# Reordering the first pair's attention, and the loads around it, in a retention-plus-mixer kernel

## The chip, the cores and the metric

The kernel runs on one core of one Trainium2 chip. The metric is the device time of one execution in microseconds (us), as the median of several runs, and lower is better. Each run also lists its mean granted TensorE clock, and 1.0 is full speed.

Short names: PE is the tensor engine, DVE VectorE, ACT ScalarE, POOL GpSimd, SP SyncE. q0 is the DMA queue that POOL's transfers use (the casting loads of the weights w1 and w2, and the stores of the output), q1 the one that SP's transfers use (loads of q, k, v, and the transposing DMAs).

## The reference

```python
# q, k, v: (8, 8, 576, 64); U: (576, 32); V: (32, 576); w_ch1: (512, 2048); w_ch2: (2048, 512)
scores = scale * np.matmul(q, k.transpose(0, 1, 3, 2))
gamma = 1.0 - 2.0 ** (-5.0 - np.arange(H))
Dmat = np.where(rel >= 0, gamma[:, None, None] ** rel[None], 0.0)   # rel = i - j
attn = np.matmul(scores * Dmat, v)
x = attn.transpose(0, 2, 1, 3).reshape(B, S, H * D)                 # (8, 576, 512)
u = x + (x.transpose(0, 2, 1) @ U @ V).transpose(0, 2, 1)           # mixing over the sequence
out = u + np.maximum(u @ w_ch1, 0.0) @ w_ch2                        # expansion, then contraction
```

## The kernel before

Batches are handled in pairs. The first pair's attention, with nothing before it to hide behind, is written out by hand in `startup` and `first_stretch`, in four units of 256 positions and two half tiles called J. From about 55 us on, a merged list runs: the two big matrix products of one pair on PE, with the attention of the next pair's chunks between them. A chunk is prepared by loads on q1, casts, and one transposing DMA:

```python
def load(pr, i, which):                     # q1: loads of a chunk's q, k, v
    ...
            nc.sync.dma_start(out=c["f", j][rows, :, :], in_=dram[...])
def xbar(pr, i):                            # q1: the chunk's transposing DMA, its output is qkT
    nc.sync.dma_start_transpose(
        out=c["qkT"], in_=c["qk"].rearrange("p j n -> p (j n)"))
def load_w1(f0, f1):                        # q0, as is load_w2
    nc.gpsimd.dma_start(out=w1_sb[:, :, w], in_=moe_w_ch1[:, w].rearrange(...))
def SC(c, pp):                              # scores of a chunk: needs qkT
    ...
            nc.tensor.matmul(pp[...], qkT[...], qkT[...], start=True, stop=True)
```

The end of the startup has the two halves of unit 1's output in one PSUM tile, with a copy (`XS_u`) after each state product (`QS_u`):

```python
RV_u(1, 1)
QS_u(1, 0, 1)
XS_u(1, 0, 1)
ST_u(1, ALL, acc2, False)
Sblk(acc2, 3)
QS_u(1, 1, 2)
XS_u(1, 1, 2)
```

In the first stretch, `y(n)` issues n expansion groups (u times a slice of w1, line L515), and w2 is loaded whole:

```python
for g in range(NI, NI + 4):                 # four chunks of the next pair
    load(*order[g], (1, 0, 2) if g < NI + 3 else (1, 0))
unit(2, (0, 1, 2), False)
y(2)
unit(3, (2, 3), True)
nc.vector.memset(w2_sb[:, 0, 0:1], 0.0)     # a marker: the loads stand behind it
for f in range(0, NF, 2):
    load_w2(f)
```

The lines named below: L514/L515 is the expansion with w1, L548/L549 the contraction with w2, L295/L296 the scores of a later chunk, L278/L279 the transposing DMA, L242/L243 the chunk loads. The lower number is with the change.

Of the kernel before, what the change touches and what calls it, by code (L numbers as in the profile page):

```python
# [9 lines left out]
FP32 = mybir.dt.float32  # L10
BF16 = mybir.dt.bfloat16
AF = mybir.ActivationFunctionType
# [22 lines left out]
def kernel(  # L35
# [11 lines left out]
    nc = tc.nc  # L47

    B, H, S, D = q.shape
    dm = H * D  # L50
# [66 lines left out]
    def early_consts():  # L117
# [26 lines left out]
        for h in range(H):  # L144
# [10 lines left out]
        nc.vector.tensor_tensor(out=posJ, in0=posJ, in1=lngt[:, 0:2, :], op=ALU.mult)  # L155
        nc.scalar.activation(out=vscaleJ, in_=posJ, func=AF.Exp, bias=lnb, scale=-1.0)
        nc.scalar.activation(out=posJ, in_=posJ, func=AF.Exp, bias=0.0, scale=1.0)
        nc.vector.tensor_scalar(
            out=triU[0:HALF], in0=iotaU[0:HALF], scalar1=0.0, scalar2=None, op0=ALU.is_ge)
        nc.vector.tensor_scalar(  # L160
# [4 lines left out]
        nc.vector.tensor_tensor(out=lngt, in0=lngt, in1=pos, op=ALU.mult)  # L165
        nc.scalar.activation(out=qscale, in_=lngt, func=AF.Exp, bias=0.0, scale=1.0)
        nc.scalar.activation(out=vscale, in_=lngt, func=AF.Exp, bias=lnb, scale=-1.0)
        nc.vector.tensor_copy(out=triH[0:HALF], in_=tri[0:HALF, 0:HALF])
        nc.vector.tensor_copy(out=triH[HALF:P], in_=tri[HALF:P, HALF:P])
        nc.vector.memset(U_E[:, J, :], 0.0)  # L170
        nc.vector.memset(U_O[0:HALF, 0, :], 0.0)
        nc.vector.memset(V4[:, 0:HALF], 0.0)
        nc.vector.memset(V4[:, HALF + S:], 0.0)
        nc.vector.tensor_copy(out=swap[:, 0:HALF], in_=ident[:, HALF:P])
        nc.vector.tensor_copy(out=swap[:, HALF:P], in_=ident[:, 0:HALF])

    def load_u_rows():
        nc.sync.dma_start(
# [53 lines left out]

    ch = {}

    def load(pr, i, which):
        c = ch.setdefault((pr, i), {})
        for j in which:
            if ("f", j) not in c:
                c["f", j] = stage.tile([P, H, D], FP32, tag="stage", name="stage_t")
            dram = (q, k, v)[j]  # L240
            for rows, b, t0 in parts(pr, i):
                n = rows.stop - rows.start  # L242
                nc.sync.dma_start(  # L243
                    out=c["f", j][rows, :, :],
                    in_=dram[b, :, t0:t0 + n, :].rearrange("h s d -> s h d"),
                )
# [383 lines left out]
    def cast_u(u, j, hh, eng):  # L630
        o, f = unit_views(u, j, hh)
        if eng is nc.scalar:
            nc.scalar.activation(out=o, in_=f, func=AF.Copy)
        else:
            eng.tensor_copy(out=o, in_=f)  # L635
# [145 lines left out]
    def zero_J(x, eng):  # L781
        for j in range(3):
            t = stage.tile([P, H, D], FP32, tag="stage", name="stage_t")
            hj[x]["f", j] = t
            if eng is nc.scalar:
                nc.scalar.activation(
                    out=t.rearrange("p h d -> p (h d)"),
                    in_=ident[:, None, :].to_broadcast([P, 4, P]), func=AF.Copy, scale=0.0)
            else:
                eng.memset(t, 0.0)  # L790
# [6 lines left out]
                out=hj[x]["f", j][0:P:2], in_=src.rearrange("h s d -> s h d"))  # L797

    def cast_J(x, eng_k, eng_q):
        t = qk_pool.tile([P, 2, dm], BF16, tag="qk", name="qk")  # L800
        hj[x]["qk"] = t
        for j, e in ((1, eng_k), (0, eng_q)):
            f = hj[x]["f", j]
            if j == 0 and x == 0:
                e.tensor_tensor(
                    out=t[:, 0, :].rearrange("p (h d) -> p h d", d=D), in0=f,
                    in1=posJ[:, 0, :, None].to_broadcast([P, H, D]), op=ALU.mult)
            elif e is nc.scalar:
                nc.scalar.activation(
                    out=t[:, j, :], in_=f.rearrange("p h d -> p (h d)"), func=AF.Copy)  # L810
            else:
                e.tensor_copy(out=t[:, j, :], in_=f.rearrange("p h d -> p (h d)"))
# [96 lines left out]
    def startup():  # L909
# [12 lines left out]
        cast_unit(0)  # L922
        T_u(0, 1, nc.vector)
        nc.vector.memset(un[0]["off"][HI], 0.0)
        zero_J(1, nc.vector)
        load_J(1, (1, 0, 2))
        load_u(2, (1, 0, 2))
# [7 lines left out]
        cast_unit(1)  # L935
        cast_u(0, 2, 0, nc.gpsimd)
        cast_u(0, 2, 1, nc.gpsimd)
        cast_u(1, 2, 0, nc.gpsimd)
        load_w1(0, 2)
        cast_u(1, 2, 1, nc.gpsimd)  # L940
        T_u(1, 1, nc.scalar)
        SC_u(0, 1, ps_o, "po")
        mask_u(0, 1)
        SC_off(0, ps_sc, "psc")
        warm(3)
        T_u(1, 0)
        nc.vector.memset(sblk, 0.0)
        SC_off(1, ps_o, "po")
        warm(3)
        SC_u(1, 0, ps_sc, "psc")  # L950
        mask_u(1, 0)
        cast_J(0, nc.scalar, nc.vector)
        SC_u(1, 1, ps_o, "po")
        mask_u(1, 1)

        acc1 = pss_tile()
        ST_u(0, ALL, acc1, True)
        Sblk(acc1, 1)
        RV_u(0, 0)
        RV_u(0, 1)  # L960
        RV_off()
        XS_u(0)
        T_J(0)
        acc2 = ps_big.tile([P, NHP, P], FP32, tag="big", name="pss2")
        ST_u(0, ALL, acc2, True)
        prep_vJ(0)
        cast_urows()
        RV_u(1, 0)
        SC_J(0)
        mask_J(0)  # L970
        ST_u(1, LO, acc1, False)
        Sblk(acc1, 2)
        cast_J(1, nc.gpsimd, nc.gpsimd)
        load_w1(2, 4)
        prep_vJ(1)
# [6 lines left out]
        load_w1(8, 10)  # L982
        for hh in range(2):
            cast_u(2, 2, hh, nc.gpsimd)
        load_w1(10, 14)
        scale_u(3, 0, nc.gpsimd)
        for hh in range(2):
            cast_u(3, 0, hh, nc.gpsimd)
        load_w1(14, 16)
        for hh in range(2):  # L990
            cast_u(3, 2, hh, nc.gpsimd)
        RV_u(1, 1)
        QS_u(1, 0, 1)
        XS_u(1, 0, 1)
        ST_u(1, ALL, acc2, False)
        Sblk(acc2, 3)
        QS_u(1, 1, 2)
        XS_u(1, 1, 2)
        RV_J(0)
        QS_J(3)  # L1000
        XS_J(0)

        xT = [ps_big.tile([P, dm], FP32, tag="big", name="xT") for _ in range(3)]
        xT.append(ps_sc.tile([P, dm], FP32, tag="psc", name="xT"))

# [27 lines left out]
    def first_stretch():  # L1033
# [21 lines left out]

        def unit(u, slots, last):
            T_u(u, 1, nc.vector)
            if last:
                y(1)
            T_u(u, 0)  # L1060
            y(1)
            SC_u(u, 0, ps_sc, "psc")
            mask_u(u, 0)
            y(1)
            ST_u(u, LO, acc, False)
            Sblk(acc, slots[1])
            SC_u(u, 1, ps_sc, "psc")
            mask_u(u, 1)
            if not last:
                scale_u(3, 1, nc.vector)  # L1070
            y(1)
            if not last:
                ST_u(u, HI, acc, False)
                Sblk(acc, slots[2])
            RV_u(u, 0)
            QS_u(u, 0, slots[0])
            QS_u(u, 1, slots[1])
            if last:
                RV_J(1)
                XS_J(1)  # L1080
            RV_u(u, 1)
            XS_u(u)

        for g in range(NI, NI + 4):
            load(*order[g], (1, 0, 2) if g < NI + 3 else (1, 0))
        unit(2, (0, 1, 2), False)
        y(2)
        unit(3, (2, 3), True)
        nc.vector.memset(w2_sb[:, 0, 0:1], 0.0)
        for f in range(0, NF, 2):  # L1090
            load_w2(f)
        y(1)
        MA1()
# [11 lines left out]
        Y1(2, 0)  # L1105
        for f in range(3):
            Y1(f, 1)
        return rest[3:]

    with tc.manual_schedule():  # L1110
# [58 lines left out]
```

## Time and profile before

| | before |
|---|---|
| median of 3 runs | 326.29 us (325.11 to 327.68) |
| span in the profile | 323.8 us |
| PE busy | 312.6 us, 97% |
| granted clock | 1.00 |
| first expansion group | 24.49 us |
| first contraction group | 72.98 us |

A line of the timeline reads: start, length, engine, line, operation, output from inputs, sizes, how many, and in brackets the idle time before it with what ended it. This is the PE timeline of before from 60 us:

```profile
59.79 6.99 PE L515 MATMUL ps_y<-uT,w_sb 128*128 128x256 bf16 x49
66.71 0.32 PE L296 MATMUL pp<-qkT 64*64 64x64 bf16 x16
...
69.64 2.77 PE L515 MATMUL ps_y<-uT,w_sb 128*128 128x256 bf16 x20 [0.65 <-ACT y L520]
...
72.98 3.19 PE L549 MATMUL ps_y<-w_sb,y 128*128 128x512 bf16 x14
```

### The profile page before, as it was taken

What the parts mean: (1) busy time and instruction counts of PE and PEld (TensorE: products, weight loads), DVE (VectorE), ACT (ScalarE), POOL (GpSimd) and SP (SyncE); (2) the same over time, 40 slices, a digit from 0 to 9 for tenths busy, and PEclk for the clock granted to TensorE, in tenths of its full rate; (3) what the DMA queues carried; (4) which work ended last, traced back from release to release, by engine and by line L of the source; (5) the groups of instructions that cost most, each with busy time, mean ns of one, the idle gap of its engine ahead of it and who ended that gap; (6) DMA issues with size and microseconds to landing.
All of it is one profiled execution on the core that took longest, in us unless ns stands there. A gap on an engine that the chain in (4) does not pass through costs nothing.

```text
span 323.8 us, 9143 instructions
## 1 busy us (share of the span) xinstructions
PE 312.6 (97%) x3885; PEld 170.8 (53%) x3885; DVE 172.9 (53%) x342; ACT 146.1 (45%) x334; POOL 101.5 (31%) x172
## 2 busy tenths in 40 slices
PE   7899899999999999999999999999999999999996
PEld 3575545764444454457644454457644454467544
DVE  7867456229726577555844476556744475500012
ACT  6757547892020583058800583058800572047400
POOL 7796329223113723052221523052231500010000
PEclk9999999999999999999999999999999999999999
DMA  7999999999975999979997599959996340330022
GB/s 215 256 233 255 227 216 185 201 188 127 254 180 139 232 193 187 213 147 190 197 205 166 140 184 206 217 140 189 182 217 156 100 68 3 107 105 0 2 78 84
DMA packets 152904, 53.30 MB, mean 165 GB/s; under 512 B 132032, under 2 KB 150336, under 8 KB 152864
## 3 DMA queue, kind: packets, MB, share of 16 engines
q1 hardware_dynamic: 144512, 40.40, 68.1%
q0 software_dynamic: 8352, 12.32, 15.9%
q8 instruction: 30, 0.49, 0.7%
q14 instruction: 10, 0.08, 0.1%
HBM read 36.85 MB, written 9.44 MB: 143 GB/s over the span
## 4 chain that ended last, share of the span: by engine, by line
PE 77%; ACT 4%; DVE 2%; DMA 1%; issue 1%; DVEq 0%
PE ps_y L549 37%; PE ps_y L515 32%; PE pp L296 2%; DVE u L464 2%; ACT y L520 1%; DMA qkT<-qk 1%; PE pp L316 1%; PE pp L328 1%; PE ps_y L560 1%; PE AB L358 1%; PE pa L431 1%; PE ph L458 1%; ACT s_sb L373 1%; ACT qk L264 0%; ACT uT L489 0%
## 5 line engine op out<-in xcount | busy, mean ns | idle before, releaser
L515 PE MATMUL ps_y<-uT,w_sb 128*128 128x256 bf16 (+2 forms) x768 | 133.1, 326 | 1.8 <-ACT y L520 1.1
L520 ACT ACTIVATE y<-ps_y 128x384 bf16<-128x384 f32 (+2 forms) x192 | 89.7, 491 | 96.6 <-PE ps_y L515 95.8
L549 PE MATMUL ps_y<-w_sb,y 128*128 128x512 bf16 x560 | 126.5, 380 | 0.0
L515 PEld LDWEIGHTS <-w_sb 128*128 128x128 bf16 x768 | 72.1, 98 | 49.6 <-issue 3.7
L549 PEld LDWEIGHTS <-y 128*128 128x128 bf16 x560 | 52.6, 98 | 61.1
L272 POOL TENSOR_TENSOR vt<-stage_t,vscale 64x256 bf16<-64x256 f32 (+1 forms) x81 | 50.4, 622 | 63.8 <-DMA stage_t<-in_v_dram 51.8
L538 DVE TENSOR_TENSOR o_sb<-ps_y,u 128x512 f32<-128x512 f32 (+2 forms) x38 | 25.2, 664 | 81.7 <-PE ps_y L549 79.4
L541 POOL DMA_DIRECT2D out_dram<-o_sb x31 | 17.2, 555 | 103.7 <-DVE o_sb L538 100.0
L304 DVE TENSOR_TENSOR ret<-pp,triH 128x512 bf16<-128x512 f32 x27 | 18.7, 692 | 24.6 <-PE pp L328 19.1
L464 DVE TENSOR_TENSOR u<-ph,xt 128x768 bf16<-128x768 f32 (+2 forms) x24 | 21.8, 951 | 5.9 <-PE ph L458 4.2
L437 ACT ACTIVATE a_sb<-pa 128x128 bf16<-128x128 f32 x8 | 2.2, 278 | 43.7 <-PE pa L431 43.7
L344 DVE TENSOR_TENSOR xt<-pp,qscale 128x512 bf16<-128x512 f32 x27 | 18.6, 690 | 4.7 <-PE pp L328 4.2
L338 DVE COPY q<-qkT 64x256 bf16<-64x256 bf16 x48 | 13.1, 272 | 13.7 <-DMA qkT<-qk 12.7
L263 DVE CAST qk<-stage_t 64x256 bf16<-64x256 f32 x54 | 18.8, 347 | 1.2
L383 DVE TENSOR_TENSOR s_sb<-AB,Af 64x256 bf16<-64x256 f32 x42 | 17.7, 422 | 2.1 <-ACT s_sb L378 1.5
L264 ACT ACTIVATE qk<-stage_t 128x512 bf16<-128x512 f32 x27 | 16.8, 622 | 0.0
L635 POOL CAST qk<-stage_t 128x512 bf16<-128x512 f32 x16 | 10.2, 637 | 11.4 <-DMA stage_t<-in_q_dram 6.6
L376 ACT ACTIVATE Af<-AB 128x256 f32<-128x256 f32 x24 | 9.2, 385 | 7.8 <-PE AB L358 7.4
L261 ACT ACTIVATE qk<-stage_t 128x256 bf16<-128x256 f32 x27 | 11.1, 410 | 0.0
L692 DVE TENSOR_TENSOR ret<-psc,triU 128x1024 bf16<-128x1024 f32 x8 | 9.6, 1206 | 2.6 <-PE psc L684 2.6
L296 PEld LDWEIGHTS <-qkT 64*64 64x64 bf16 x432 | 5.6, 107 | 9.8 <-issue 8.0
L209 PE MATMUL pw<-ident 128*128 128x512 bf16 x26 | 7.8, 443 | 1.4 <-POOL ident masks.py:199 1.4
(134 smaller groups left out, 220.0 us busy)
## 6 DMA issues: line engine op xcount, KB each, us to landing
stage_t<-in_k_dram SPq DMA_DIRECT2D x32, 256.0 KB, 4.9
stage_t<-in_q_dram SPq DMA_DIRECT2D x32, 256.0 KB, 5.4
stage_t<-in_v_dram SPq DMA_DIRECT2D x32, 256.0 KB, 5.6
out_dram<-o_sb POOLq DMA_DIRECT2D x31, 256.0 KB, 3.5
w_sb<-in_moe_w_ch_dram POOLq DMA_DIRECT2D x14, 256.0 KB, 8.3
stage_t<-in_k_dram SPq DMA_DIRECT2D x8, 128.0 KB, 3.7
stage_t<-in_q_dram SPq DMA_DIRECT2D x8, 128.0 KB, 3.7
stage_t<-in_v_dram SPq DMA_DIRECT2D x8, 128.0 KB, 3.9
```

What stands on the lines that cost most here:

```text
L263: nc.vector.tensor_copy(out=o[to, hl], in_=f[fr, hl])
L264: nc.scalar.activation(out=c["qk"][:, 0, :], in_=c["f", 0].rearrange("p h d -> p (h d)"), func=AF.Copy)
L272: nc.gpsimd.tensor_tensor(out=o[to, hl], in0=f[fr, hl], in1=w[fr, hl, :, None].to_broadcast([n, NHP, D]), op=ALU.mult)
L304: nc.vector.tensor_tensor(out=ret.rearrange("p a b i -> p a (b i)").rearrange("p a (b i) -> p a b i", i=D), in0=pp[:, :, 0:NHP * D].rearra ...
L344: nc.vector.tensor_tensor(out=st["x", pr][:, i, :].rearrange("p (hp hl d) -> p hl hp d", hl=2, d=D), in0=pp[:, :, NHP * D:2 * NHP * D].rea ...
L383: nc.vector.tensor_tensor(out=S_[half(x), 1, :], in0=Bk[half(1 - x)], in1=Af[half(1 - x), now, :], op=ALU.add)
L464: nc.vector.tensor_tensor(out=st["u", par][:, i0 - base:i0 - base + n, w].rearrange("p s (c d) -> p c s d", c=2), in0=ph[k][:, :, 0:n, :], ...
L515: nc.tensor.matmul(ps[:, 0:n, :], w1_sb[:, cc, f * P:(f + 1) * P], st["uT", par][:, c0:c0 + n, cc, :], start=(cc == 0), stop=(cc == NCC - 1),)
L520: nc.scalar.activation(out=st["y1", par][:, f, c0 * P:(c0 + n) * P], in_=ps[:, 0:n, :].rearrange("p s t -> p (s t)"), func=AF.Relu)
L538: nc.vector.tensor_tensor(out=o_sb[:, 0:n], in0=ps[:, 0:n], in1=st["u", par][:, c, w], op=ALU.add)
L541: (nc.sync if last else nc.gpsimd).dma_start(out=out_flat[r0:r0 + P, w], in_=o_sb[:, 0:n])
L549: nc.tensor.matmul(ps, st["y1", par][:, f, c * P:(c + 1) * P], w2_sb[:, f, :], start=(f == 0), stop=(f == NF - 1),)
```

## The change

The intent: shorten the startup, where two copies stand in a row with a matmul between them, and let the late q loads of unit 3 land sooner by keeping other transfers out of their way. The core of the diff (constants, memsets and signatures cut):

```diff
         SC_u(1, 0, ps_sc, "psc")
         mask_u(1, 0)
-        cast_J(0, nc.scalar, nc.vector)
...
+        T_J(0)
         RV_u(0, 0)
         RV_u(0, 1)
         RV_off()
         XS_u(0)
...
+        RV_u(1, 0)
+        RV_u(1, 1)
+        ST_u(1, ALL, acc2, False)
+        Sblk(acc2, 3)
+        QS_u(1, 0, 1)
+        QS_u(1, 1, 2)
+        XS_u(1)
...
-        load_w1(10, 14)
-        scale_u(3, 0, nc.gpsimd)
-        for hh in range(2):
-            cast_u(3, 0, hh, nc.gpsimd)
+        scale_u(3, 0, nc.gpsimd)
+        cast_u(3, 0, 0, nc.gpsimd)
+        load_w1(10, 14)
+        cast_u(3, 0, 1, nc.gpsimd)
         load_w1(14, 16)
+        load(*order[NI], (1,), gate=nc.gpsimd)
...
             T_u(u, 1, nc.vector)
-            if last:
-                y(1)
+            y(1)
             T_u(u, 0)
...
-        y(2)
+        y(1)
         unit(3, (2, 3), True)
         nc.vector.memset(w2_sb[:, 0, 0:1], 0.0)
-        for f in range(0, NF, 2):
+        for f in range(0, NF // 2, 2):
             load_w2(f)
...
             Y1(f, 1)
+        nc.scalar.activation(
+            out=w2_sb[:, NF // 2, 0:1], in_=ident[:, 0:1], func=AF.Copy)
+        for f in range(NF // 2, NF, 2):
+            load_w2(f)
```

"The attention" is the startup's new order and its early constants, with w1's slices 10 to 16 behind casts. "The gate" is the POOL memset ahead of the first chunk's k load, which holds the chunk loads behind w1. "The y move" is the expansion group that moves into unit 2. "The split" is w2's second half behind a marker on ACT at the end of the first stretch.

More of the change, by code (lines that the diff above doesn't have):

```diff
@@ L157, in early_consts @@
         nc.scalar.activation(out=posJ, in_=posJ, func=AF.Exp, bias=0.0, scale=1.0)
+        nc.scalar.activation(out=triH[0:HALF], in_=tri[0:HALF, 0:HALF], func=AF.Copy)
+        nc.scalar.activation(out=triH[HALF:P], in_=tri[HALF:P, HALF:P], func=AF.Copy)
+        nc.scalar.activation(out=swap[:, 0:HALF], in_=ident[:, HALF:P], func=AF.Copy)
+        nc.scalar.activation(out=swap[:, HALF:P], in_=ident[:, 0:HALF], func=AF.Copy)
         nc.vector.tensor_scalar(
@@ L167, in early_consts @@
         nc.scalar.activation(out=vscale, in_=lngt, func=AF.Exp, bias=lnb, scale=-1.0)
-        nc.vector.tensor_copy(out=triH[0:HALF], in_=tri[0:HALF, 0:HALF])
-        nc.vector.tensor_copy(out=triH[HALF:P], in_=tri[HALF:P, HALF:P])
-        nc.vector.memset(U_E[:, J, :], 0.0)
-        nc.vector.memset(U_O[0:HALF, 0, :], 0.0)
-        nc.vector.memset(V4[:, 0:HALF], 0.0)
-        nc.vector.memset(V4[:, HALF + S:], 0.0)
-        nc.vector.tensor_copy(out=swap[:, 0:HALF], in_=ident[:, HALF:P])
-        nc.vector.tensor_copy(out=swap[:, HALF:P], in_=ident[:, 0:HALF])
+        nc.vector.memset(sblk, 0.0)
     def load_u_rows():
@@ L233, with load @@
     ch = {}
-    def load(pr, i, which):
+    def load(pr, i, which, gate=None):
         c = ch.setdefault((pr, i), {})
@@ L239, in load @@
                 c["f", j] = stage.tile([P, H, D], FP32, tag="stage", name="stage_t")
+            if gate is not None:
+                gate.memset(c["f", j][:, 0:1, 0:1], 0.0)
             dram = (q, k, v)[j]
@@ L799, in cast_J @@
     def cast_J(x, eng_k, eng_q):
-        t = qk_pool.tile([P, 2, dm], BF16, tag="qk", name="qk")
-        hj[x]["qk"] = t
+        if "qk" not in hj[x]:
+            hj[x]["qk"] = qk_pool.tile([P, 2, dm], BF16, tag="qk", name="qk")
+        t = hj[x]["qk"]
         for j, e in ((1, eng_k), (0, eng_q)):
+            if e is None:
+                continue
             f = hj[x]["f", j]
@@ L924, in startup @@
         nc.vector.memset(un[0]["off"][HI], 0.0)
+        nc.vector.memset(U_E[:, J, :], 0.0)
+        nc.vector.memset(U_O[0:HALF, 0, :], 0.0)
+        nc.vector.memset(V4[:, 0:HALF], 0.0)
+        nc.vector.memset(V4[:, HALF + S:], 0.0)
         zero_J(1, nc.vector)
@@ L937, in startup @@
         cast_u(0, 2, 1, nc.gpsimd)
+        cast_J(0, None, nc.gpsimd)
         cast_u(1, 2, 0, nc.gpsimd)
+        cast_u(1, 2, 1, nc.gpsimd)
         load_w1(0, 2)
-        cast_u(1, 2, 1, nc.gpsimd)
         T_u(1, 1, nc.scalar)
@@ L946, in startup @@
         T_u(1, 0)
-        nc.vector.memset(sblk, 0.0)
         SC_off(1, ps_o, "po")
-        warm(3)
+        cast_J(0, nc.scalar, None)
         SC_u(1, 0, ps_sc, "psc")
         mask_u(1, 0)
-        cast_J(0, nc.scalar, nc.vector)
-        SC_u(1, 1, ps_o, "po")
-        mask_u(1, 1)
         acc1 = pss_tile()
@@ L958, in startup @@
         Sblk(acc1, 1)
+        SC_u(1, 1, ps_o, "po")
+        mask_u(1, 1)
+        acc2 = ps_big.tile([P, NHP, P], FP32, tag="big", name="pss2")
+        ST_u(0, ALL, acc2, True)
+        T_J(0)
         RV_u(0, 0)
@@ L962, in startup @@
         XS_u(0)
-        T_J(0)
-        acc2 = ps_big.tile([P, NHP, P], FP32, tag="big", name="pss2")
-        ST_u(0, ALL, acc2, True)
-        prep_vJ(0)
-        cast_urows()
-        RV_u(1, 0)
         SC_J(0)
@@ L972, in startup @@
         Sblk(acc1, 2)
+        prep_vJ(0)
+        cast_urows()
+        RV_u(1, 0)
[5 more added lines that the diff above has]
+        XS_u(1)
+        RV_J(0)
+        QS_J(3)
+        XS_J(0)
         cast_J(1, nc.gpsimd, nc.gpsimd)
@@ L984, in startup @@
             cast_u(2, 2, hh, nc.gpsimd)
+        scale_u(3, 0, nc.gpsimd)
+        cast_u(3, 0, 0, nc.gpsimd)
         load_w1(10, 14)
-        scale_u(3, 0, nc.gpsimd)
-        for hh in range(2):
-            cast_u(3, 0, hh, nc.gpsimd)
+        cast_u(3, 0, 1, nc.gpsimd)
         load_w1(14, 16)
+        load(*order[NI], (1,), gate=nc.gpsimd)
         for hh in range(2):
             cast_u(3, 2, hh, nc.gpsimd)
-        RV_u(1, 1)
-        QS_u(1, 0, 1)
-        XS_u(1, 0, 1)
-        ST_u(1, ALL, acc2, False)
-        Sblk(acc2, 3)
-        QS_u(1, 1, 2)
-        XS_u(1, 1, 2)
-        RV_J(0)
-        QS_J(3)
-        XS_J(0)
         xT = [ps_big.tile([P, dm], FP32, tag="big", name="xT") for _ in range(3)]
@@ L1084, in first_stretch @@
         for g in range(NI, NI + 4):
-            load(*order[g], (1, 0, 2) if g < NI + 3 else (1, 0))
+            load(*order[g], ((0, 2) if g == NI else (1, 0, 2)) if g < NI + 3 else (1, 0))
         unit(2, (0, 1, 2), False)
-        y(2)
+        y(1)
         unit(3, (2, 3), True)
         nc.vector.memset(w2_sb[:, 0, 0:1], 0.0)
-        for f in range(0, NF, 2):
+        for f in range(0, NF // 2, 2):
             load_w2(f)
```

## The prediction

> **What bounds the kernel now.** I read the page first, then the waits of the tensor engine (PE), then the timeline of the first 80 us, then the DMA queues in short windows. The page says where time can be had at all:
>
> ```profile
> span 323.8 us, 9143 instructions
> PE 312.6 (97%) x3885; PEld 170.8 (53%) x3885; DVE 172.9 (53%) x342; ACT 146.1 (45%) x334; POOL 101.5 (31%) x172
> PE   7899899999999999999999999999999999999996
> PEclk9999999999999999999999999999999999999999
> ```
>
> PE is idle 323.8 - 312.6 = 11.2 us. Busy time by stretch splits them: 6.1 before 67 us, 0.7 from 67 to 110, 1.4 from 110 to 300, 3.0 in the last stretch. The change touches nothing that runs after about 75 us, and 1.4 of the first 6.1 us wait for the identity matrix at the very start, which stays. It removes three of the 26 warming matmuls (L209), 0.65 us by their pitch. So the most that is open to it is 6.1 + 0.7 - 1.4 + 0.65 = 6.0 us, and 2% of 326.29 is 6.5. What the rest waits for is in the waits of PE (total us, times, longest):
>
> ```profile
> PE pst L655 <- POOL qk L635: 1.1, 1, 1.1
> PE ps_y L515 <- ACT y L520: 1.1, 3, 0.6
> PE po L711 <- DVE ret L692: 0.5, 1, 0.5
> PE psx L726 <- DVE ret L692: 0.5, 1, 0.5
> PE po L746 <- DVE xt L754: 0.3, 1, 0.3
> ```
>
> The startup (to the first expansion matmul, L515) is the first pair's attention. Its warming matmuls (L209) run in waits and hide them. The timeline (start, length, count, idle before and its releaser) shows the chain that sets the end of this stage:
>
> ```profile
> 13.63 0.82 PE L209 MATMUL pw<-ident 128*128 128x512 bf16 x3
> 14.38 0.86 PE L684 MATMUL psc<-qkT 64*64 64x128 bf16 x32
> 21.00 0.40 PE L746 MATMUL po<-sblk,qkT 128*128 128x128 bf16 x4 [0.34 <-DVE xt L754]
> 22.47 0.46 PE L431 MATMUL pa<-xt,U_E 128*32 128x128 bf16 x20
> 24.49 1.11 PE L515 MATMUL ps_y<-uT,w_sb 128*128 128x512 bf16 x4
> ```
>
> The second state product (L746, slot 2) waits until VectorE (DVE) has copied the first half of the output (L754, 20.25 to 20.94) because both halves are one PSUM tile; a second copy (21.43 to 22.12) then releases the mixer's product L431 at 22.47. Two copies of 0.69 us stand in a row with a matmul between them.
>
> In the next stage (24.5 to 55 us) the largest wait is 1.14 us before 38.74: the transposes of unit 3 need a GpSimd (POOL) cast (38.06 to 38.68) of a query half issued at about 26 and landing only at 38.0. The DMA queues of the window 50 to 55 us (packets, MB, share of engine time) show the other contest, w2 (q0) against the chunk loads (q1):
>
> ```profile
> q0 software_dynamic: 721, 0.70, 88.2%
> q1 hardware_dynamic: 853, 0.22, 26.0%
> ```
>
> [...] from 50 to 55 us w2 moves 0.70 MB and the loads 0.22 MB, where the loads alone moved 0.96 MB from 45 to 50. [...] a 64x64 bf16 copy on DVE (triH) took 1.03 us beside a 2.07 us POOL scaling, while a 128x64 one later took 0.18 us. [...] One group of warming matmuls goes, which leaves at most 0.7 us of idle, and the granted clock reads 1.00 in every stretch; I expect no change.
>
> **The change part by part.**
>
> (a) The early constants. Two triH and two swap copies go from DVE to ScalarE (ACT), which stands idle 1.71 us before qscale at 5.01; four copies at an estimated 0.2 us each (from its 0.21 us activation of 8 columns) fit. The zeroing of sblk (0.91 us) goes from 14.26 to about 5, and small memsets move later. DVE gains about 0.3: the first mask starts at 10.53 behind the zeroing L790 (9.04 to 10.61), though its scores are done at 10.18; it should start at 10.25. With that the off product, the transposes of unit 1 and the scores at 14.38 come 0.28 earlier: 14.10. Removing three warming matmuls (0.82) gives nothing: the scores wait for the copy of the transposes (DVE 13.39 to 14.12) anyway.
>
> (b) The first mask of unit 1 no longer waits behind the sblk memset (14.26 to 15.17), and the cast of q of J (0.69 on DVE between two masks) is now 1.04 us on POOL, by the other two-tensor operations there. Masks of 1.2 us then end at 15.7 and 16.9 instead of 16.26 and 17.99.
>
> (c) The new PE order from 14.10, by the pitches of the timeline (8 transposes or state sums 0.55, 16 scores 0.35, 32 products 0.57, 16 off products 0.48, 8 J scores 0.27, 4 state products 0.22): scores 14.45, sums 15.0, scores 15.35, sums 15.9, J transposes 16.45, products 17.0, off 17.5, J scores 17.8, sums 18.25, unit 1 products 18.8, sums 19.35, first state product 19.55. ACT: T_J 16.5 to 17.45, slot 2 18.3 to 19.05 (0.78), slot 3 19.4 to 20.15. So the second state product ends at 19.8, waiting for nothing. DVE: output copy of unit 0 17.55 to 18.75 (needs (b)), J masks to 19.5, then the one copy of both halves of unit 1 (1.21 by L754 in its wide form) 19.8 to 21.0. J's part ends on ACT at 21.15. The mixer product starts at 21.1 instead of 22.47: -1.35. The rest of the chain keeps its lengths, so the first L515 group starts at 24.49 - 1.35 = 23.1. w1's first slice is issued at 16.3 instead of 15.42 and lands near 21, in time.
>
> (d) In unit 2 an expansion group (1.0 us) now lies between its two transposes groups, hiding the 0.34 us copy wait at 28.46. Against it, unit 2's values are cast only at 30.0 (DMA landing 29.4), and PE will be there at 29.7: 0.3 is given back. Net 0.
>
> (e) Unit 3 and w1. w1 (10 to 14) was issued at 29.94; behind the cast of unit 3's first q half (34.76) it goes at 35.4. Before about 34.3 nothing changes, as q0 was still moving earlier slices (1.31 of 2.1 MB by then). From 34.3 to 38 q0 moved 0.5 MB and q1 only 0.3: without it the second q half should land at 36.2, not 38.0. PE reaches these transposes at 37.6 - 1.35 - 0.3 = 36.0 and waits until 36.8 instead of 38.74. So -1.9 there. But PE then reaches group f10 at 40.3, and its w1 slice of 0.5 MB, begun at 37.4 beside unit 3's values, lands at about 41: 0.6 comes back. Left after (a) to (e): about -1.3 to -1.9, say -1.6.
>
> (f) The gate on the chunk loads costs nothing: they stood behind unit 3's loads in the same ring, and the first landed at 41.5 (issue 30.51, 11.0 us). w2's later half frees DMA between 50 and 57, but POOL's value scalings (first at 52.51) now stand behind its issue and begin at about 58; they are needed at 65, so 5 us are to spare. PE's wait here is small (ACT y 1.1 in three, a transposing DMA 0.4); gain 0 to 0.3.
>
> Sum: 326.29 - 1.6 - 0.2 = 324.5.
>
> **The rivals.** *A data-bound second stage*: POOL and DMA set units 2 and 3, so PE arriving 1.35 us early only waits longer; if q still lands at 38, the gain ends there and the time is about 326.1. For it: landing times of 7 to 11.6 us in that stage; against it: q0's share of 77 to 81% from 34 to 38, which is just what moves. *w1 becomes the wait*: the later issue of slices 10 to 16 makes expansion groups wait up to 2 us; 326.5. For it: a landing of 10.1 us for the 512 KB slice; against it: no chunk loads beside it now. *More than I count*: the w2 split removes also the waits at 66 to 70 (1.05 us) and the w1 wait does not come; 322.8. [...]
>
> **Range and chances.** The first stage is worked out from durations and I trust it to 0.4 us; the second rests on DMA shares, to 1 us; the three runs of before spread 325.11 to 327.68, so a median of three may be off by 0.7. Eight in ten: 322.9 to 326.2. Faster by over 2% would need 319.8, more than the 6.0 us that are open: 0.02. Slower by over 2% would need a 6.5 us stall that nothing here suggests: 0.02. The rest, 0.96, is within 2%.
>
> **What would show it.** Right: one L754 copy of 1.21 us for unit 1 ending near 21.0, L431 at 21.1, first L515 at 23.1, no wait L746 on L754; the wait of L655 on POOL L635 below 1 us and ending near 36.8; L515 after 60 us about 1.6 us earlier in place. Wrong: the first L515 earlier but the transposes of unit 3 still near 38.7 (rival one); L515 waiting for the DMA of w_sb by over 1 us (rival two); a new wait of L847 or L711 on ACT or POOL in 16 to 20 us, if the J chain is longer than I put it.

The memset of sblk took 0.91 us in before and in after.

## More of the kernel before

```profile
46.90 5.62 POOL L218 DMA_DIRECT2D w_sb<-in_moe_w_ch_dram  x8 [5.51 <-DVE w_sb L1089]
```

All eight loads of w2 are issued from 46.90, and the first transposing DMA at 60.24. The DMA view of the window 62 to 66 us of before (packets, MB, share of the engines' time; last line: median us from issue to landing):

```profile
q1 hardware_dynamic: 2207, 0.55, 87.6%
q0 software_dynamic: 257, 0.24, 35.6%
...
qkT<-qk SPq DMA_TRANSPOSE x1, 6.4
```

w2 is almost through: in windows of 1 us its q0 moves 0.15 MB from 62 to 63, 0.07 from 63 to 64, 0.01 from 64 to 65. The transposing DMA lands at 66.6, just before PE comes at 66.71.

The timelines of SP's and POOL's DMA issues of before show which transfers meet there:

```profile
60.24 4.33 SPq L279 DMA_TRANSPOSE qkT<-qk  x1
```

## The result, and the profile after

After took 330.06 us median of six runs (328.16 to 330.58), against 326.27 of six runs of before: ratio 1.0101, 95% interval 1.0063 to 1.0138. It is 1% slower, outside the predicted range and in the other direction. A ratio here and below is the mean time of one kernel's fast runs over that of the other's fast runs beside it, so it is not quite the ratio of the medians. Clocks of the six runs were 0.988 to 0.994. From the page of after:

```profile
span 328.4 us, 9130 instructions
...
PE   7897999959999999999999999999999999999996
...
PEclk9999999989999999999999999999999999999999
...
PE 74%; DMA 6%; ACT 3%; DVE 2%; issue 1%; DVEq 0%
```

The ninth slice (65.7 to 73.9 us) holds all the news: PE is half busy where it was full, the clock is down, and in the chain that ended last (the last line) DMA has 6% where it had 1%. The PE timeline of after, startup and second stage:

```profile
21.51 0.46 PE L430 MATMUL pa<-xt,U_E 128*32 128x128 bf16 x20
...
23.53 1.10 PE L514 MATMUL ps_y<-uT,w_sb 128*128 128x512 bf16 x4
...
27.83 1.04 PE L514 MATMUL ps_y<-uT,w_sb 128*128 128x512 bf16 x4 [1.11 <-DMA w_sb<-in_moe_w_ch_dram]
...
31.33 1.04 PE L514 MATMUL ps_y<-uT,w_sb 128*128 128x512 bf16 x4 [0.41 <-DMA w_sb<-in_moe_w_ch_dram]
```

The startup is shorter by 24.49 - 23.53 = 0.96 us. Then the third and fifth expansion groups wait 1.11 and 0.41 us for slices of w1, and the gain is gone: before began its seventh expansion group near 34.27 + 0.95 = 35.2 (half of a row of two groups), after at 35.84. The removed wait for unit 3's transposes (1.14 us in before) brings it back in part. The scores of unit 3 start at 39.83 against 40.08, and PE is 0.25 us ahead at 54. Then, in the PE timeline of after from 60 us:

```profile
59.81 6.72 PE L514 MATMUL ps_y<-uT,w_sb 128*128 128x384 bf16 x47
70.32 0.32 PE L295 MATMUL pp<-qkT 64*64 64x64 bf16 x16 [3.80 <-DMA qkT<-qk]
...
70.70 6.19 PE L514 MATMUL ps_y<-uT,w_sb 128*128 128x384 bf16 x32
...
77.46 2.76 PE L548 MATMUL ps_y<-w_sb,y 128*128 128x512 bf16 x12
```

The scores start 3.61 us later than in before (70.32 against 66.71), and the 32 matmuls after them take 6.19 us, where before had them, its ACT wait included, from 67.08 to 72.41. The first contraction is at 77.46 against 72.98: 4.48 us later, of a span that is 4.6 longer. So everything is lost between 60 and 77 us. The windows view shows why the 32 matmuls are slow (busy us of each engine with counts, then granted clock, DMA share, GB/s):

```profile
71.00:72.00 1.00, 1.00 (x9) 0.69 (x7) 0.96 (x3) 0.98 (x4) 0.33 (x1) 0.80 1.39 184
72.00:75.00 3.00, 3.00 (x12) 1.64 (x11) 0.43 (x1) 1.51 (x4) 1.51 (x3) 0.50 1.35 203
```

PE is fully busy, but the granted clock is 0.50 from 72 to 75 us. The DMA issues in the timelines of after, SP's and POOL's:

```profile
59.99 3.83 SPq L278 DMA_TRANSPOSE qkT<-qk  x1
```

```profile
57.36 2.80 POOL L215 DMA_DIRECT2D w_sb<-in_moe_w_ch_dram  x4 [7.91 <-ACT w_sb L1111]
```

The transposing DMA is issued 0.25 us earlier than before, but w2's second half was issued just ahead of it. The DMA view of the window 62 to 66 us of after:

```profile
q0 software_dynamic: 608, 0.59, 122.1%
q1 hardware_dynamic: 605, 0.15, 50.0%
...
qkT<-qk SPq DMA_TRANSPOSE x1, 10.3
```

Where w2 was nearly done, it now moves 0.59 MB, and q1 falls from 0.55 to 0.15 MB. The transposing DMA takes 10.3 us instead of 6.4. A hole shows further up: in 34 to 38 us all queues moved 0.93 MB in before and 0.62 MB in after. In before q0 moved 0.52 MB of it and in after 0.08, since slices of w1 are issued later. The gate keeps the chunk loads from filling the hole: without it (attn_only below) all queues moved 0.83 MB there.

### The profile page after: what moved, and what is told of

Its sections match the earlier page's. It is cut to its first block, busy times and chain, and to the rows that moved or that the text cites. A ratio compares the mean times of both kernels' runs of the same rounds, so it can differ in the third digit from the quotient of the medians.

```text
span 328.4 us, 9130 instructions
## 1 busy us (share of the span) xinstructions
PE 314.0 (96%) x3882; PEld 171.5 (52%) x3882; DVE 171.1 (52%) x336; ACT 146.9 (45%) x339; POOL 101.8 (31%) x174
## 4 chain that ended last, share of the span: by engine, by line
PE 74%; DMA 6%; ACT 3%; DVE 2%; issue 1%; DVEq 0%
PE ps_y L548 35%; PE ps_y L514 31%; DMA qkT<-qk 5%; PE pp L295 2%; DVE u L463 2%; DMA uT<-u 1%; PE pp L315 1%; ACT y L519 1%; PE ps_y L559 1%; PE pp L327 1%; PE AB L357 1%; PE pa L430 1%; PE ph L457 1%; ACT s_sb L372 0%; ACT uT L488 0%
## 5 line engine op out<-in xcount | busy, mean ns | idle before, releaser
L514 PE MATMUL ps_y<-uT,w_sb 128*128 128x256 bf16 (+2 forms) x768 | 134.8, 329 | 2.8 <-DMA w_sb<-in_moe_w_ch_dram 1.5
L295 PE MATMUL pp<-qkT 64*64 64x64 bf16 x432 | 8.6, 198 | 4.3 <-DMA qkT<-qk 4.3
```

Of the source, the lines that this page charges most:

```text
L295: nc.tensor.matmul(pp[half(m), m ^ hl, hp * D:(hp + 1) * D], qkT[half(hl), NHP + hp, half(m)], qkT[half(hl), hp, half(m ^ hl)], start=True ...
L514: nc.tensor.matmul(ps[:, 0:n, :], w1_sb[:, cc, f * P:(f + 1) * P], st["uT", par][:, c0:c0 + n, cc, :], start=(cc == 0), stop=(cc == NCC - 1),)
```

## The experiments

Theory A: w2's second half beside the first transposing DMA of the next pair is what holds it, and PE pays for the wait and for the half clock after it. Rival B: the gate makes the chunk loads, and with them the transposing DMA, late. Rival C: loads ahead of it in its own queue hold it. Rival D: the y move and w1's slices. All kernels gave a correct result. They ran in four batches, the last two on one chip; "before" ran beside each, with medians of 325.92 to 326.51. The last batch (whole_yback, best_c, best_d) is held against twelve runs of before, of which eleven are those of the batch ahead of it. In the text, T is the first transposing DMA of the next pair. All the measurements first, for the comparison (low clock: how many runs had under 0.997; medians in us of all runs; the three columns of T in us, from the one profiled run):

| kernel | median | ratio, 95% interval | low clock | T issued | T took | PE's wait for it |
|---|---|---|---|---|---|---|
| before | 326.27 | 1 | see below | 60.24 | 6.4 | none |
| after | 330.06 | 1.0101, 1.0063 to 1.0138 | 6 of 6 | 59.99 | 10.3 | 3.80 |
| after_again | 329.69 | 1.0085, 1.0035 to 1.0134 | 4 of 4 | 59.80 | 11.3 | 4.84 |
| w2_whole | 327.96 | 1.0047, 0.9990 to 1.0104 | 1 of 4 | 65.21 | 3.9 | 1.74 |
| no_gate | 327.25 | 1.0020, 0.9971 to 1.0070 | 1 of 4 | 60.47 | 8.2 | 1.76 |
| split_only | 327.07 | 1.0023, 0.9965 to 1.0082 | 1 of 4 | 61.02 | 8.4 | 1.89 |
| warm_in_stall | 329.39 | 1.0074, 1.0021 to 1.0128 | 0 of 4 | 59.23 | 10.2 | 0.68 |
| w2_late | 331.12 | 1.0157, 1.0124 to 1.0189 | 4 of 4 | 59.77 | 3.3 | none |
| c12_behind | 329.62 | 1.0102, 1.0057 to 1.0147 | 3 of 4 | 60.53 | 9.1 | 2.59 |
| y_back | 329.13 | 1.0089, 1.0018 to 1.0159 | 3 of 4 | 60.04 | 9.4 | 2.91 |
| attn_only | 325.81 | 0.9995, 0.9963 to 1.0028 | 0 of 4 | 60.23 | 6.9 | 0.39 |
| w2_behind_T | 333.16 | 1.0198, 1.0155 to 1.0241 | 4 of 4 | 59.02 | 4.2 | none |
| best_a | 333.09 | 1.0198, 1.0159 to 1.0236 | 6 of 6 | 61.01 | 3.3 | none |
| best_b | 331.96 | 1.0168, 1.0130 to 1.0207 | 6 of 6 | 60.08 | 3.3 | none |
| whole_yback | 327.89 | 1.0034, 0.9990 to 1.0077 | 2 of 4 | 64.94 | 4.0 | 2.69 |
| best_c | 327.77 | 1.0030, 0.9989 to 1.0072 | 2 of 6 | 61.19 | 6.3 | 1.38 |
| best_d | 325.89 | 0.9982, 0.9940 to 1.0024 | 1 of 6 | 63.65 | 3.9 | 1.01 |

A low clock was not after's alone: of before's own runs, one of seven in the first of these batches and three of twelve in the last had 0.995, and took 327.79 to 329.12 us.

### One part undone or alone

**w2_whole** is after with w2 issued whole, as before.

```diff
-        for f in range(0, NF // 2, 2):
+        for f in range(0, NF, 2):
             load_w2(f)
...
-        nc.scalar.activation(
-            out=w2_sb[:, NF // 2, 0:1], in_=ident[:, 0:1], func=AF.Copy)
-        for f in range(NF // 2, NF, 2):
-            load_w2(f)
```

> The changed kernel with w2 issued whole again, behind the marker on VectorE, as before; all else as changed. Theory A (w2's second half, issued at 57 to 60 us, shares the DMA engines with the first transposing DMA of a chunk, so that this lands 10.3 us after its issue instead of 6.4, PE stands 3.8 us and its clock then falls to 0.50 for 4 us): the transposing DMA lands within 7 us, PE's wait for it is below 1.5 us, the clock stays 1.00, and the time is 325.0 to 326.5. Theory B (the chunk loads, held back by the gate until 38.6 us instead of 30.5, stand in front of the transposing DMA in its own queue): w2 is not the cause, the wait stays above 3 us and the time stays at 329 to 331, or is worse, as w2 then blocks the late loads.

1.0047: about half of the loss is gone, in the mean. The transposing DMA now took 3.9 us, but it was issued only at 65.21. SP was held at the issue of a chunk load from 60.40 to 65.03: the gate had moved the chunk loads back into w2. PE waited 1.74 us. Neither forecast came whole: T was as fast as theory A had it, but the wait and the time were above its figures, and below those of rival B.

**no_gate** is after without the gate; the chunk loads are issued as in before.

```diff
-        load(*order[NI], (1,), gate=nc.gpsimd)
...
-            load(*order[g], ((0, 2) if g == NI else (1, 0, 2)) if g < NI + 3 else (1, 0))
+            load(*order[g], (1, 0, 2) if g < NI + 3 else (1, 0))
```

> The changed kernel without the gate: the first chunk's key load is issued with the others, as before; w2 stays in two halves. Theory A: nothing is won, PE's wait for the transposing DMA stays at 3 to 4 us, the clock falls, the time is 329 to 331. Theory B: the loads are in front by some 7 us, the transposing DMA has an empty queue ahead of it, lands within 7 us, and the time is 325.0 to 326.5.

1.0020. The transposing DMA was issued at 60.47 and took 8.2 us; PE waited 1.76 us. Again the result lies between the two forecasts. So each of the two parts makes PE wait when the other is taken away, and neither makes the whole wait. That either costs time by itself is not shown, as both intervals reach below 1.

**split_only** is the kernel before with the split alone.

```diff
-        for f in range(0, NF, 2):
+        for f in range(0, NF // 2, 2):
             load_w2(f)
...
+        nc.scalar.activation(
+            out=w2_sb[:, NF // 2, 0:1], in_=ident[:, 0:1], func=AF.Copy)
+        for f in range(NF // 2, NF, 2):
+            load_w2(f)
```

> The kernel before with nothing changed but w2's second half issued later (marker on ScalarE). Theory A: this alone makes the loss: PE waits 3 to 4 us for the first transposing DMA, the clock falls after it, and the time is 329.5 to 331.5. Theory B: the loads are as early as before, so the wait stays near 0.4 us and the time at 326.3.

1.0023, so the cost in time is not shown by itself, but the wait that it brings is: 1.89 us, where theory A had 3 to 4 and theory B 0.4. The profiled run, the slowest of the four (329.28), happened to be the one with the low clock. Its PE timeline, the DMA view of 62 to 66 us, and its windows:

```profile
69.44 0.32 PE L296 MATMUL pp<-qkT 64*64 64x64 bf16 x16 [1.89 <-DMA qkT<-qk]
...
69.82 6.20 PE L515 MATMUL ps_y<-uT,w_sb 128*128 128x384 bf16 x32
```

```profile
q0 software_dynamic: 598, 0.58, 103.3%
q1 hardware_dynamic: 6, 0.00, 0.3%
```

```profile
71.00:74.00 3.00, 3.00 (x13) 1.68 (x12) 0.55 (x1) 1.62 (x5) 1.62 (x3) 0.50 1.34 196
```

The first scores slip from 66.71 to 69.44 with nothing changed but the split. While w2 moves 598 packets, q1 moves six, although the transposing DMA has been issued at 61.02. The wait of 1.89 us was followed by half clock (0.50) from 71 to 74. Its runs at clock 1.0 took 326.51, 326.53 and 327.6, so the run with the half clock is 1.7 to 2.8 us longer, with whatever else differed in it.

**warm_in_stall** is after with 14 warming matmuls ahead of the late scores, so that the stall stays but PE does not idle.

```diff
             c = ch[pr, n]
+            if pr == 1 and n == 0:
+                warm(14)
             SC(c, pp)
```

> The changed kernel with 14 warming matmuls (0.216 us each, 3.0 us in all) put on PE just ahead of the first score matmuls of the second pair, where it waits 3.8 us for the transposing DMA. They do no work for the result. If the fall of the clock after the wait (matmuls of 71 to 75 us at half rate) costs what the trace suggests, some 1.7 us, the wait shrinks below 1 us, the clock stays 1.00, and the time falls from 330.1 to about 328.4. If the half clock is not paid for on the path (other waits would take its place), the time stays at 330.

The clock stayed at 0.999 to 1.0 in all four runs, and the 32 matmuls took 4.52 us instead of 6.19. The ratio was 1.0074, against 1.0101 and 1.0085 of after in other batches. So by the means at most 0.9 us was won, less than expected, and the intervals overlap; the profiled run was the fastest of the four. By the means, most of the loss is the stall itself.

**y_back** is after with the groups of unit 2 where they were, and **c12_behind** is after with the fourth chunk's k and q loads issued behind the transposing DMA instead of ahead of it.

```diff
             T_u(u, 1, nc.vector)
-            y(1)
+            if last:
+                y(1)
...
-        y(1)
+        y(2)
         unit(3, (2, 3), True)
```

> The changed kernel with the expansion groups of unit 2 where they were (none between its two transposes, two behind it). The third group is then asked for about 1 us later: its wait for w1, 1.1 to 1.8 us in four profiles, falls by 0.6 to 1, the copy wait of 0.34 us returns. If PE's place in the second stage decides, the time falls by 0.3 to 0.6 us; if the transposing DMA at 70 us decides (its landing does not depend on PE), PE only waits longer there and the time stays at 329 to 331. I expect the latter.

1.0089, with the wait for w1 still 1.28 and 0.85 us and the wait for the transposing DMA 2.91. The y move is not the cause; with attn_only below, which keeps w1's later slices, this answers rival D.

```diff
-        for g in range(NI, NI + 4):
+        for g in range(NI, NI + 3):
...
-            [(0.04, ready(0)), (0.05, fetch(3, (2,))),
+            [(0.04, ready(0)), (0.045, fetch(3, (1, 0))), (0.05, fetch(3, (2,))),
```

> The changed kernel with the key and query loads of the fourth chunk issued behind the first transposing DMA instead of ahead of it; gate and w2 in halves stay. If the transposing DMA is held up by what stands ahead of it in its own queue (0.5 MB of 256-byte packets, at some 0.1 MB in 2 us while w2 has the engines), it lands within 7 us of its issue at 59 to 60, PE's wait falls from 3.8 to below 1 us, the clock stays 1.00 and the time is 325.5 to 327.5. If only w2's share beside it counts, the wait stays at 3 us or more and the time at 329 to 330.

1.0102, landing still 9.1 us; PE's wait was 2.59 us. From 62 to 66 us q1 moved only 86 packets, while q0 moved 0.57 MB. Here, loads ahead of it in its own queue are not what holds it (rival C). The time says less, as this run also waited 1.43 us for the second transposing DMA.

**attn_only** is the change without the gate, the split and the y move. Its edit is the three above together.

> The changed kernel without gate, with w2 whole and the expansion groups where they were: left of the change are the reordered attention, the early constants and the later issue of w1's slices 10 to 16. The start of the expansion stays at 23.3 to 23.6 us instead of 24.5. If the gain of 1 us at the start is kept, the time is 324.8 to 325.8. If the second stage and the first transposing DMA are bound by the DMA engines, whose work is the same, PE arrives early and waits, and the time is 326 to 327.

0.9995, clock 1.0 in all four runs: the loss is gone, and no gain is left either. The waits of PE of attn_only (total us, times, longest):

```profile
PE ps_y L514 <- DMA w_sb<-in_moe_w_ch_dram: 1.1, 2, 0.6
...
PE pss L762 <- POOL qk L634: 0.8, 1, 0.8
PE pp L295 <- DMA qkT<-qk: 0.7, 2, 0.4
```

Its first expansion group was at 23.28, which is 1.21 us earlier than before. It then waited 1.1 us for w1 and 0.8 us for a POOL cast, and its first contraction was at 73.04 (before: 72.98).

### Moving w2's second half away from the transposing DMA

**w2_late** is after with the second half issued after the first chunk's section.

```diff
+        def w2_rest():
+            nc.vector.memset(w2_sb[:, NF // 2, 0:1], 0.0)
+            for f in range(NF // 2, NF, 2):
+                load_w2(f)
...
-             ... (0.20, ready(2)),
+             ... (0.215, w2_rest), (0.20, ready(2)),
```

> The changed kernel with the marker for w2's second half put on VectorE behind the first section of the second pair, so that these four transfers can start only after the first transposing DMA has landed. After the first four runs the theory (A with B) is: this transposing DMA lands when all that stands beside it and ahead of it has drained; w2's second half beside it costs some 2 us, the hole that the gate leaves in the DMA engines at 34 to 42 us costs some 2 more[...]. Here only the first is taken away, more fully than in w2_whole: from 62 to 66 us the loads' queue moves over 0.4 MB instead of 0.15, the transposing DMA lands by 66, PE's wait is below 1 us and the clock stays 1.00. The time is 325.5 to 327.0, unless the second half now comes late for the projection, which would show as a wait of the L548 matmuls for w_sb and give up to 1.5 us back. The rival (the held-back loads alone decide) keeps the wait at 3 us and the time at 329 to 330.

The time was a miss, but it is the cleanest test of the theory. The DMA view of 59 to 63 us of w2_late, then its PE timeline and the waits of PE:

```profile
q1 hardware_dynamic: 2708, 0.68, 82.4%
qkT<-qk SPq DMA_TRANSPOSE x1, 3.3
```

```profile
66.23 0.32 PE L295 MATMUL pp<-qkT 64*64 64x64 bf16 x16
...
72.50 1.90 PE L548 MATMUL ps_y<-w_sb,y 128*128 128x512 bf16 x7
```

```profile
PE ps_y L548 <- DMA w_sb<-in_moe_w_ch_dram: 3.0, 4, 1.0
```

Same kernel, gate and all, but no w2 beside it: the transposing DMA lands in 3.3 us instead of 10.3, PE does not wait, and the first contraction is at 72.50, 0.48 us ahead of before. Then w2 itself comes too late, in four waits of 3.0 us in all, and the clock fell in all four runs (0.990 to 0.995).

**w2_behind_T** issues the second half as soon as the first transposed chunk has landed.

```diff
+        def w2_rest():
+            nc.gpsimd.tensor_copy(
+                out=w2_sb[:, NF // 2, 0:1], in_=ch[order[NI]]["qkT"][:, 0, 0:1])
+            for f in range(NF // 2, NF, 2):
+                load_w2(f)
...
+             ... (0.10, w2_rest), ...
```

> The changed kernel with one edit: w2's second half is issued as soon as the first transposing DMA of the next pair has landed (behind a small copy that reads the transposed chunk), not ahead of it. Theory A (the second half of w2 beside the transposing DMA is what holds it): the transposing DMA, issued near 60, lands within 4 us; no wait of PE on it above 0.5 us near 66 to 70; the clock stays at 1.0 in every run; w2 lands some 8 us later, near 72, before the first group that reads its second half or under 1 us late; time 325.5 to 327.5. Rival B (the transposing DMA is slow because of what the gate moved: chunk loads late, holes in the engines): landing of 7 us or more and a wait above 1.5 us stay; time 328.5 or more.

333.16 us: far off what theory A expected in time, within 0.2 us of each of its steps up to 66 us, and then the stall came back one transposing DMA later. Its SP timeline, the DMA view of 59 to 63 us, the DMA view of 64 to 72 us, and the PE timeline:

```profile
59.02 2.26 SPq L278 DMA_TRANSPOSE qkT<-qk  x1
...
64.88 1.26 SPq L278 DMA_TRANSPOSE qkT<-qk  x1
```

```profile
qkT<-qk SPq DMA_TRANSPOSE x1, 4.2
```

```profile
qkT<-qk SPq DMA_TRANSPOSE x2, 11.0
```

```profile
65.49 0.32 PE L295 MATMUL pp<-qkT 64*64 64x64 bf16 x16
...
76.99 0.43 PE L295 MATMUL pp<-qkT 64*64 64x64 bf16 x16 [5.80 <-DMA qkT<-qk]
```

The first one took 4.2 us. The second, issued at 64.88 beside w2's second half (issued at 63.92), landed 12.07 us later by the chain, and PE waited 5.80 us for it. I had asked when the first would land, and not what came next in that queue. Five chunk loads stood ahead of the second one in its queue, but in w2_late the same five stood ahead of it, it was issued at 64.71, ahead of w2's half (67.62), and it took 3.8 us. So this shows the same a second time, on another chunk: in after the transposing DMA that met w2 was the first (10.3 us), here the second (12.07).

**best_a** and **best_b** were candidates. best_a is w2_behind_T without the gate and the y move, and with the fourth chunk's loads behind the first transposing DMA. best_b has w1's slices nearer to their use as well:

```diff
-        cast_J(1, nc.gpsimd, nc.gpsimd)
         load_w1(2, 4)
+        cast_J(1, nc.gpsimd, nc.gpsimd)
...
+        load_w1(10, 12)
         scale_u(3, 0, nc.gpsimd)
         cast_u(3, 0, 0, nc.gpsimd)
-        load_w1(10, 14)
+        load_w1(12, 14)
```

> A candidate: the change without the gate on the chunk loads and with the y groups of unit 2 where they were, the second half of w2 and the fourth chunk's loads behind the first transposing DMA. Theory A: no wait on the transposing DMA, clock 1.0 in every run, the early gain of about 1 us partly kept, since the wait for w1's slices (about 1.3 us) stays: 324.6 to 326, ratio 0.995 to 0.999. Rival (the second stage is bound by the bytes of w1 and gives all of the early gain back): 326, ratio 1.000.

> best_a, and w1's slices nearer to their use: slice 2 to 4 issued ahead of the first casts of the J halves, 10 to 12 ahead of a scaling, 12 to 14 behind the first cast of the last unit. If the order of POOL's own issues is what makes the slices late, the wait of the third y group (1.1 to 1.8 us elsewhere) falls below 0.5 us and the time to 324 to 325.2, ratio 0.993 to 0.997. If the engines' bytes bound the slices, the wait is as long as in best_a or moves to another operand, and the time is that of best_a within 0.5 us.

Both fail for the same reason as w2_behind_T: PE waits 5.30 and 4.29 us for the second transposing DMA near 77 us, which took 10.3 and 9.2 us. The wait for w1 went as best_b's first reading had it (1.5 us in best_a, none listed in best_b), but the time did not follow. Here moving w2's half behind one transposing DMA did not help, because another follows, and moving it further (w2_late) made w2 itself late.

> The changed kernel itself, as a control on the chip of these runs: 328.5 to 331, ratio 1.006 to 1.014, the transposing DMA landing 9 to 11 us after its issue, PE waiting 3 to 4 us for it, clock 0.988 to 0.995 in most runs.

The control agrees in time: 1.0085, clocks 0.990 to 0.995. The landing of 11.3 us and the wait of 4.84 are somewhat above the forecast.

### What is left without the split

What was then open: why the attention alone ends level, and what the gate costs.

> The changed kernel with w2 whole and the y groups where they were: what is left is the attention and the gate. If the gate by itself costs, 327 to 328.5, ratio 1.003 to 1.007, as with w2 whole alone (1.0047): the chunks' loads land 1 to 3 us late, the transposing DMA is issued near 63 to 65, PE waits 1.5 to 2 us. If it was the moved y groups, 326 to 326.7, ratio 0.999 to 1.002.

**whole_yback** (the attention and the gate; the edits of w2_whole and y_back) came to 1.0034. As with w2_whole, SP was held at a chunk load until 64.75 and issued the transposing DMA at 64.94, which took 4.0 us; PE waited 2.69. The wait is longer than the 1.5 to 2 us of the forecast. Against attn_only, which differs from it by the gate alone, T is issued 4.7 us later and PE waits 2.30 us more. So the gate makes PE wait by making the chunk loads late, as rival B has it. The interval just includes 1, and in its four runs the clock fell twice.

**best_c** is attn_only with best_b's order of w1. **best_d** is best_c with the next pair's attention begun a little later.

```diff
-            mixing(2, 0.16, 0.70, (0.71, 0.77)),
+            mixing(2, 0.19, 0.71, (0.71, 0.77)),
```

> The attention reordered alone (no gate, w2 whole, y groups as before), and w1's slices issued nearer to their use. If the order of POOL's own issues is what makes the slices late, the waits for w1 (1.1 us together with the attention alone) fall below 0.3 us and no other wait grows, 324.5 to 325.3, ratio 0.994 to 0.998. If POOL or the engines bound the second stage, the wait moves to POOL's casts of the later units and the time is that of the attention alone, 325.6 to 326.4, ratio 0.998 to 1.001.

> best_c with the next pair's attention section begun a little later (at 0.19 of the list instead of 0.16, some 1 to 2 us). If the landing of the first transposing DMA is what sets the end of the early part, PE's wait on it (0.4 us with the attention alone, more if PE comes earlier) goes to zero and 0.3 to 1 us are won against best_c. If something else is, the time is that of best_c within 0.3 us, or worse by the attention that is squeezed later.

The waits of PE of best_c from 20 to 80 us:

```profile
PE pp L295 <- DMA qkT<-qk: 2.2, 2, 1.4
PE pst L654 <- POOL qk L634: 1.0, 1, 1.0
PE pss L762 <- POOL qk L634: 0.6, 2, 0.4
```

The waits for w1 are gone. In their place stand 1.6 us for POOL's casts of later units: this fits the second reading, that the wait moves. The time of best_c (327.77) is above both readings. With w2 whole and no gate the transposing DMA lands near 67 whatever PE does: at 66.6 in before, 67.1 in attn_only, 67.5 in best_c and best_d. PE's early arrival turns into a wait there. best_d was to take that wait to zero; it was still 1.01 us, and 0.87 more for the second one. best_d reached 0.9982; its interval includes 1 and overlaps that of best_c, so no version is shown to beat the kernel before, and the gain of best_d over best_c is not shown either.

## Why the prediction was wrong, point by point

**Step (a), 0.3 us: did not come in this profile.** The first mask was to start at 10.25. It started at 10.84, still behind the zeroing (9.38 to 10.95), since four memsets had moved ahead of it, and since its scores came at 10.16 instead of 9.76 (POOL had waited 0.52 us for a k load). In other profiles with the same startup the mask began between 10.18 (w2_late) and 10.98 (whole_yback), and in split_only, which has the startup of before, at 10.84. So it varies from profile to profile by more than the 0.3 us at stake.

**Steps (b) and (c): right.** The -1.35 us held the 0.28 of step (a), so about 1.1 was theirs. From the scores of unit 1 to the first expansion group I had 23.1 - 14.1 = 9.0 us. It took 23.53 - 14.60 = 8.93 us, against 24.49 - 14.38 = 10.11 in before: 1.18 won. The one wide copy took 1.22 us and ended at 21.45, and no state product waited for a copy.

**Step (d), "Net 0": wrong, by about 1.5 us.** I weighed only unit 2's values against it. The waits of 1.11 and 0.41 us for w1 were not in my sum. They are the sign that I had named for rival two, though on slices earlier than those that I watched, and not for its reason: the slice that the third group needs was issued at 20.03 and took 7.8 us, against 19.80 and 7.7 in before. It landed as before, and PE came for it earlier. Nor does the y move make these waits, which y_back and attn_only have without it. attn_only and best_c show why trading them is no use: without the w1 waits PE waits for POOL's casts.

**Step (e), -1.9 and 0.6 back: mechanism right, size wrong.** The wait for unit 3's transposes went, and that part of the change did what it was for: POOL cast the second q half at 37.20 instead of 38.06. But PE no longer came there early, so only some 0.9 us was won (0.6 behind at the seventh group, 0.25 ahead at the scores of unit 3). The 0.6 that I expected back at the later slices did not come. In all, -1.6 was predicted for this part of the run and -0.25 was measured at 54 us: my rival one was nearly right about what is left, though not for its reason, since the q half did land earlier.

**Step (f), "The gate on the chunk loads costs nothing" and "gain 0 to 0.3": this is the step that failed.** It held the whole of the loss. I had quoted the contest of w2 with q1 in the window 50 to 55 us, and saw the split as making room there. I did not ask what the second half would run beside 10 us later. I had also misread the waits. The 0.4 us for a transposing DMA that I put here, and counted again among "the waits at 66 to 70 (1.05 us)", is in the waits of the whole span; in before the only such wait of PE is at 268.44 us. Near 66 us there was none, and the ACT wait near 70 us was 0.65. So the first transposing DMA, which I took to be harmless, was the one transfer without slack. It landed some 1 to 3 us after w2 was through in before, attn_only, after and split_only, and in 3.3 to 4.2 us where no w2 was beside it (w2_late, w2_behind_T, best_a, best_b). With the split beside it, it took 8.2 to 11.3 us; with w2 whole ahead of it, 3.9 to 6.9. The sum for after: 3.61 us at the scores, then 0.87 up to the first contraction (77.46 - 72.98 = 4.48), in which the half clock costs about 6.19 - 4.52 = 1.7 us and before's own 0.65 us wait is no longer there.

**The gate.** Undone alone it takes after from 1.0101 to 1.0020; left alone with the attention it stands at 1.0034, against 0.9995 without it. The split undone gives 1.0047. All of these intervals but that of after include 1. What is shown is that after is slower, that it is level without these parts and the y move (1.0101 and 0.9995, with intervals apart), and that y_back changes little. How the 1% divides between gate and split is about half and half by the means, no more than that. PE's wait for T tells the same more clearly, with one profile each: 0.39 us with neither (attn_only, which lacks the y move too), 1.74 with the gate alone (w2_whole), 1.76 with the split alone (no_gate), 3.80 with both (after). They work in different ways. With w2 whole the gate moved the issue of T from 60.23 (attn_only) to 64.94 (whole_yback); with the split it did not (59.99 in after, 60.47 in no_gate), and q1 moved more beside w2 instead (605 packets from 62 to 66 us in after, 73 in no_gate), while T took 2 us longer.

**"I expect no change" of the clock: right for its reason, wrong in result.** The removed warming matmuls left the clock at 1.00 up to 70 us. It fell to 0.50 after the 3.80 us stall of step (f), and stayed at 0.999 to 1.0 when warming matmuls filled that stall (warm_in_stall). In split_only a single wait of 1.89 us was followed by clock 0.50 from 71 to 74 us, while the profiled runs of best_c and whole_yback, with waits of 1.38 and 2.69 us, had a mean clock of 1.0. So the runs show no length of wait from which it falls.

**Range and chances.** "Slower by over 2% would need a 6.5 us stall that nothing here suggests" held in size, but a stall of 3.8 us came. My range ended at 326.2, 0.1 us below the time of before, because I took every part of the change to be harmless at worst.

**Still open.** Why a transposing DMA makes so little progress beside w2 is not settled. Plain loads did not stand back in this way here. Before T was issued, the chunk loads moved 629 packets beside 641 of w2; this is attn_only from 54 to 58 us:

```profile
q0 software_dynamic: 641, 0.62, 91.3%
q1 hardware_dynamic: 629, 0.16, 29.5%
```

Nor is it only that w2 takes all the bandwidth: from 63 to 64 us in split_only q0 moved 52 packets (0.05 MB), and q1 still none. No run here had a plain load in T's own place, or w2 with other packets.

## What to carry to other kernels

Before moving a large load later, list what is issued in the stretch that it moves into, and find the transfer there that lands just before its use; an existing wait of near zero is no sign of slack (in before, T landed at 66.6 us and PE came at 66.71). Look up where a wait stands before placing it in a stage; a sum over the span does not say. Where transposing DMAs follow one another, as here, moving a weight load behind one only puts it beside the next (12.07 us for the second in w2_behind_T). A gain in a startup lasts only if the next stage has slack: look at which transfer lands at a fixed time whatever PE does (T here, at 66.6 to 67.5 us with w2 whole and no gate).
